# Moving weight loads to the K queue in a fixed order, and keeping V loads in order with the exps, in a grouped-query attention kernel

## The chip, the cores and the metric

The kernel runs on one core of a Trainium2 chip. The metric is the device time of one execution in microseconds. Several executions are measured, and each has a state, fast or slow (here slow means more than 1.5% above the fastest run of the same kernel). Times are medians of all runs. A profile is one further look at one execution; its span is about 2 us shorter than the time reported for it (757.7 against 759.44 us before).

## The reference, cut to what matters

Two independent problems A and B of the same shape are computed, and their outputs are concatenated.

```python
B, Sq, D = 16, 80, 576                 # batch, queries, model width
Hq, Hkv, Sk, Dh = 32, 16, 512, 128     # two query heads share a K/V head
q = (x @ wq).reshape(B, Sq, Hq, Dh).transpose(0, 2, 1, 3)
k, v = repeat(k_cache, 2, axis=1), repeat(v_cache, 2, axis=1)
p = softmax(einsum("bhqd,bhkd->bhqk", q, k) * Dh ** -0.5)
o = einsum("bhqk,bhkd->bhqd", p, v)
out = o.transpose(0, 2, 1, 3).reshape(B, Sq, Hq * Dh) @ wo
```

Everything is bf16. Each problem reads 33.6 MB of K, as much of V, 4.7 MB of wq and 4.7 MB of wo.

## The kernel before: the parts that matter

The work is cut into 128 *units*. A unit is one batch entry and four K/V heads (512 KB of K, 512 KB of V). Eight units make an *octet*, which shares one quarter of wq and of wo (1.18 MB each). There are 16 octets: 0 to 7 are problem A, 8 to 15 are B. In program order a unit is: K loaded with a transposing DMA (from SP), V loaded (from ScalarE, "ACT"), V converted by GpSimd ("POOL"), scores on TensorE, exp on ScalarE, P·V on TensorE, transposes, output projection.

Every operation is recorded with a key (the intended position, 16 key steps to a unit) and its reads and writes. A planner then simulates all engines with estimated costs and fixes the order of each engine's instructions. The program gives each engine its instructions in that order. In the timelines below, what stands behind a slow DMA issue of the same engine waits for it: ScalarE's first table load comes at 25.38 us, when its last DMA issue of that stretch ends.

```python
NK = 5      # K buffers
NV = 2      # V input buffers
NVP = 4     # converted V buffers
...
    def _simulate(self, ops, alldeps):
        ...     # at each step: the engine that can go first takes the ready op with the lowest key
            if o.dsem is not None:                       # a DMA
                free[e] = t0 + self.ISSUE[e]
                kind = o.name.rstrip("0123456789.")
                link = max(link, free[e] + 0.6) + self.XFER[kind]
                end, lat = link, 1.3
...
        # K and V loads of unit U
        t_k = T0 - 16.0 * (NK - 1) - LA + 1.5 if U >= NK else -790.0 + 3 * U
        t_p = T0 - 24.0 if U >= 2 else -700.0 + U
        t_v = t_p - 16.0 * NV + 1.0 if U >= NV else -789.0 + 3 * U
        add("sp", t_k, em_ldk, writes=[R(("kT", ks), U)], dsem="d_k%d" % ks, name="ldk%d" % U)
        add("act", t_v, em_ldv, writes=[R(("Vi", vs), U)], dsem="d_v%d" % vs, name="ldv%d" % U)
        add("pool", t_p, em_vp, reads=[R(("Vi", vs), U), ...], writes=[R(("V", vps), U)], name="vp%d" % U)
...
        # weights: wq in three pieces, wo in two, per problem and quarter q, on ScalarE
                    add("act", t_w + dt * part, em_ldwa, ...)
            add("sp" if (prob, q) == (0, 0) else "act", t_w + 2 * dt, em_ldwb, ...)
                add("act", t_wo + 24.0 * part, em_ldwo, ...)
```

A weight load has no predecessor while its buffer is free. The planner therefore places it as early as the engine's simulated time allows, whatever its key says.

Of the kernel before, what the change touches and what calls it, by code (L numbers as in the profile page):

```python
# [616 lines left out]
class _Plan(_Sched):  # L617
# [13 lines left out]
    def plan(self):  # L631
        ops = sorted(self.ops, key=lambda o: (o.key, o.seq))
        last_w, readers, cur_ver = {}, {}, {}
        alldeps = {}
        for op in ops:
            deps = {}
            for r, ver in op.reads:
                w = last_w.get(r)
                assert w is not None, ("read of never-written resource", r, op.name)
                assert cur_ver[r] == ver, ("version mismatch", r, cur_ver[r], ver, op.name)  # L640
                deps[id(w)] = w
            for r, ver in op.writes:
                w = last_w.get(r)
                if w is not None:
                    deps[id(w)] = w
                for rd in readers.get(r, ()):
                    deps[id(rd)] = rd
            deps.pop(id(op), None)
            for r, ver in op.reads:
                readers.setdefault(r, []).append(op)  # L650
            for r, ver in op.writes:
                last_w[r] = op
                readers[r] = []
                cur_ver[r] = ver
            alldeps[id(op)] = list(deps.values())
            for d in deps.values():
                if d.eng == "pe" and op.eng == "pe":
                    continue
                op.deps.append(d)
                d.signals = True  # L660
            if op.dsem is not None:
                op.signals = True
        order = self._simulate(ops, alldeps)
        for i, op in enumerate(order):
            op.key, op.seq = float(i), i
        counts = {}
        for op in order:
            if not op.signals:
                continue
            ck = ("d", op.dsem) if op.dsem is not None else ("e", op.eng)  # L670
            counts[ck] = counts.get(ck, 0) + (16 if op.dsem is not None else 1)
            op.sidx = (ck, counts[ck])
        self.totals = counts
        known = {}
        for op in order:
            kq = known.setdefault(op.eng, {})
            need = {}
            for d in op.deps:
                ck, v = d.sidx
                if need.get(ck, (0, None))[0] < v:  # L680
                    need[ck] = (v, d)
            for ck, (v, d) in sorted(need.items(), key=lambda kv: -kv[1][1].key):
                if kq.get(ck, 0) >= v:
                    continue
                op.waits.append((ck, v))
                for k2, v2 in d.clock.items():
                    if kq.get(k2, 0) < v2:
                        kq[k2] = v2
            if op.signals:
                op.clock = dict(kq)  # L690
                op.clock[op.sidx[0]] = op.sidx[1]
        self.sorted_ops = order
        return order

    def _simulate(self, ops, alldeps):
        ndep = {id(o): len(alldeps[id(o)]) for o in ops}
        users = {}
        for o in ops:
            for d in alldeps[id(o)]:
                users.setdefault(id(d), []).append(o)  # L700
        ready = {id(o): 0.0 for o in ops}
        cand = {}
        for o in ops:
            if not ndep[id(o)]:
                cand.setdefault(o.eng, []).append(o)
        free = {e: 0.0 for e in ("pe", "act", "dve", "pool", "sp")}
        link = 0.0
        order = []
        self.pe_idle = []
        lastdma = {}  # L710
        while any(cand.values()):
            best = None
            for e, cs in cand.items():
                if not cs:
                    continue
                t0 = max(free[e], min(ready[id(o)] for o in cs))
                if best is None or t0 < best[0]:
                    best = (t0, e)
            t0, e = best
            cs = cand[e]  # L720
            o = min((o for o in cs if ready[id(o)] <= t0 + 1e-9), key=lambda o: (o.key, o.seq))
            cs.remove(o)
            if e == "pe" and t0 > free[e] + 0.02:
                self.pe_idle.append((t0 - free[e], t0, o.name))
            o.clock = t0
            order.append(o)
            if o.dsem is not None:
# [4 lines that stand above are left out]
            else:  # L732
                free[e] = t0 + self.cost[id(o)]
                end, lat = free[e], self.LAT.get(e, 0.1)
            for u in users.get(id(o), ()):
                same = u.eng == e and o.dsem is None
                t = t0 if same and e == "pe" else end + (0.06 if same else lat)
                ready[id(u)] = max(ready[id(u)], t)
                ndep[id(u)] -= 1
                if not ndep[id(u)]:  # L740
                    cand.setdefault(u.eng, []).append(u)
        self.span = max(free.values())
        assert len(order) == len(ops)
        for o in order:
            o.clock = None
        return order


def bass_concat_heads__gqa_block_cached__gqa_block_cached__near_ridge_kernel(
# [61 lines left out]
    def R(res, ver):  # L811
        return (res, ver)
# [39 lines left out]
    for ph in range(NPH):  # L852
        prob, half = divmod(ph, NPP)
# [38 lines left out]
    for prob in range(2):  # L892
        wq_ap, wo_ap = probs[prob][3], probs[prob][4]
        u_p = prob * NPP * SUPP
        for q in range(NOCT):
            if prob == 0:
                t_w = (-799.0, -785.0, 16.0 * 5 + 10.0, 16.0 * 12 + 10.0)[q]
            else:
                t_w = 16.0 * (u_p - SUPP + 8 * q + 4) + 10.0
            dt = (0.1 if q == 1 else 0.4) if prob == 0 and q < 2 else 6.0  # L900
            if (prob, q) == (0, 0):
                for hp in range(4):
                    def em_ldwp(e, wq_ap=wq_ap, hp=hp):
                        src = wq_ap[0:512, hp * 256:(hp + 1) * 256]
                        return e.dma_start(wq_sb[:, 0, 0:4, hp * 256:(hp + 1) * 256],
                                           src.rearrange("(c p) n -> p c n", p=128))

                    add("act", t_w + 0.1 * hp, em_ldwp, writes=[R(("wq", 0, p_, hp), 0) for p_ in range(2)],
                        dsem="d_wp%d" % hp, name="ldwp%d" % hp)
            else:  # L910
                for part, (c0, c1) in enumerate(((0, 2), (2, 4))):
                    def em_ldwa(e, wq_ap=wq_ap, q=q, c0=c0, c1=c1):
                        src = wq_ap[c0 * 128:c1 * 128, q * 1024:(q + 1) * 1024]
                        return e.dma_start(wq_sb[:, q, c0:c1, :], src.rearrange("(c p) n -> p c n", p=128))  # L914

                    add("act", t_w + dt * part, em_ldwa, writes=[R(("wq", q, part, hp), prob) for hp in range(4)],
                        dsem="d_wq%d" % q, name="ldwa%d.%d.%d" % (prob, q, part))

            def em_ldwb(e, wq_ap=wq_ap, q=q):
                return e.dma_start(wq_sb[64:128, q, 4, :], wq_ap[512:576, q * 1024:(q + 1) * 1024])  # L920

            add("sp" if (prob, q) == (0, 0) else "act", t_w + 2 * dt, em_ldwb,
                writes=[R(("wq", q, 2, hp), prob) for hp in range(4)], dsem="d_wq%d" % q, name="ldwb%d.%d" % (prob, q))
            for part in range(2):
                h0 = 8 * q + 4 * part

                def em_ldwo(e, wo_ap=wo_ap, h0=h0):
                    src = wo_ap[h0 * 128:(h0 + 4) * 128, :]
                    return e.dma_start(wo_sb[:, h0:h0 + 4, :], src.rearrange("(h p) n -> p h n", p=128))  # L929

                t_wo = 16.0 * (u_p + 8 * q) - 40.0 if u_p + q else 14.0
                add("act", t_wo + 24.0 * part, em_ldwo, writes=[R(("wo", q, part), prob)],
                    dsem="d_wo%d" % q, name="ldwo%d.%d.%d" % (prob, q, part))


    for k in range(2 * NPH * NOCT):
        goct, c = divmod(k, 2)
        ph, q = divmod(goct, NOCT)
# [270 lines left out]
    ops = S.plan()  # L1209
# [79 lines left out]
```

## Time and profile before

Median 758.85 us of three runs (757.82 to 769.3, the last one slow). The profiled run's span is 757.7 us.

To see where time goes, the span is cut at the first P·V matmul of every eighth unit. The P·V line of the trace has 16 matmuls per unit, so the cut times are start times read from it. An octet that nothing disturbs takes about 41.5 us.

| stretch of the span, us | before |
|---|---|
| start to unit 0's first P·V | 39.0 |
| octet 0 | 53.4 |
| octets 1, 2 | 41.7, 41.8 |
| octets 3 to 8 | 43.8, 45.4, 49.3, 43.5, 48.9, 47.4 |
| octets 9 to 14 | 41.5, 42.4, 43.2, 41.4, 42.4, 41.6 |
| from unit 120 to the end | 51.0 |

The page's busy table and its slices. Each digit is the busy share of one fortieth of the span in tenths; PEclk is the granted TensorE clock in tenths.

```profile
PE 700.5 (92%) x9508; PEld 593.8 (78%) x9508; DVE 386.2 (51%) x961; ACT 382.2 (50%) x732; POOL 244.8 (32%) x136
...
PE   4387999999999897999989989999999999999986
...
ACT  0163565555555553554535546555555566555561
...
PEclk8589999999999998999999989999999999999999
DMA  9998999999999999999999989998999998989941
```

TensorE is the engine that is full, except in the first four slices and in a handful near the middle. ScalarE does nothing in the first slice and little in the second.

The timeline of the first 45 us (start, duration, engine and line, what; in brackets the idle time before it and its releaser). "ACTq" and "SPq" are issues by ScalarE's and SP's sequencers.

```profile
9.08 39.28 SPq L1022 DMA_TRANSPOSE kT<-in_A_k_cache_dram  x4
9.13 7.30 ACTq L929 DMA_DIRECT2D wo_sb<-in_A_wo_dram  x3
...
16.46 3.40 ACTq L914 DMA_DIRECT2D wq_sb<-in_A_wq_dram  x2
...
21.96 3.39 ACTq L914 DMA_DIRECT2D wq_sb<-in_A_wq_dram  x2
25.38 1.28 ACT L960 ACT_TABLE_LOAD   x1 [25.38 <-issue]
...
26.67 0.43 ACT L960 CAST qT<-ps 128x320 bf16<-128x320 f32 x1
...
27.16 5.25 PE L953 MATMUL ps<-xT,wq_sb 128*128 128x320 bf16 x20 [16.66 <-ACT qT L960]
```

ScalarE issues weights (and two V loads) until 25.4 us. Only then does it copy the first query projection out of PSUM (the tile `ps`, which the matmuls write), and TensorE has stood for 16.66 us. Meanwhile four K issues on SP take 39 us together.

From the waits view (total us, times, longest) and, second, the chain of waits (start, duration, what):

```profile
POOL v_sb L1029 <- DMA v_in<-in_A_v_cache_dram: 123.8, 28, 30.8
...
ACT P L994 <- POOL v_sb L1029: 26.3, 8, 5.5
...
PE ps L989 <- ACT P L994: 22.1, 14, 4.4
...
PE ps L953 <- ACT qT L960: 16.7, 1, 16.7
```

```profile
281.27 14.84 DMA v_in<-in_A_v_cache_dram
...
379.18 10.40 DMA v_in<-in_A_v_cache_dram
...
423.46 12.69 DMA v_in<-in_B_v_cache_dram
```

In the middle the chain runs through V loads that land after 10 to 15 us (the median for V is 5.6 us). In octets 3 to 8 TensorE's gaps add up to 16.0 us, of which 15.8 us are waits for ScalarE's exps ("ACT P" in the waits view of 175.9 to 454.2 us). ScalarE itself stands until GpSimd has converted a late V (26.3 us in eight waits), because its next instruction is the V load into that buffer. Within about 1 us of the end of each of the three longest gaps (299.1, 392.7 and 439.2 us) a stretch begins in which the granted TensorE clock is 0.50 (298.3, 393.8 and 438.2 us); these are 17.1 us in all, and TensorE is busy in 15.2 of them. In such a stretch, from the start of one group to the start of the next, five projection matmuls took 1.34 us and eight output matmuls 1.92 us (299.94 to 303.20 us); at full clock they took 0.68 and 0.98 us (306.65 to 308.31 us). That is about half the work, so the stretches cost another 7.6 us (an estimate: half of the 15.2 busy us).

### The profile page before, as it was taken

How to read it: one execution, taken by the hardware profiler on the slowest of the kernel's cores; microseconds unless marked ns; L12 is line 12 of the kernel's file. 1: busy time of each engine (PE TensorE's matmuls, PEld its weight loads, DVE VectorE, ACT ScalarE, POOL GpSimd, SP SyncE). 2: the span in 40 equal slices, each digit the busy share in tenths (PEclk: the TensorE clock that was granted, in tenths of full speed). 3: DMA queues.
4: the chain of work that ended last, by engine and by line, in shares of the span. 5: the costliest groups of instructions: out<-in, count | busy, mean ns of one | idle time of the engine just before them, and what ended most of it. 6: DMA issues, size and time to landing. Idle time of an engine off the chain costs nothing.

```text
span 757.7 us, 21437 instructions
## 1 busy us (share of the span) xinstructions
PE 700.5 (92%) x9508; PEld 593.8 (78%) x9508; DVE 386.2 (51%) x961; ACT 382.2 (50%) x732; POOL 244.8 (32%) x136
## 2 busy tenths in 40 slices
PE   4387999999999897999989989999999999999986
PEld 3265788888888786887878868888888888888874
DVE  1023456555655443555646525555665545655564
ACT  0163565555555553554535546555555566555561
POOL 4012353322432322323324224323433324332230
PEclk8589999999999998999999989999999999999999
DMA  9998999999999999999999989998999998989941
GB/s 259 301 303 175 214 235 199 212 215 200 204 230 259 183 212 229 216 266 259 253 245 233 219 190 189 225 205 201 187 202 202 216 229 196 199 207 204 200 93 38
DMA packets 355142, 161.08 MB, mean 213 GB/s; under 512 B 269536, under 2 KB 350944, under 8 KB 355040
## 3 DMA queue, kind: packets, MB, share of 16 engines
q1 hardware_dynamic: 272528, 73.75, 56.2%
q10 hardware_dynamic: 82512, 85.86, 41.5%
q8 instruction: 77, 1.26, 0.7%
q14 instruction: 25, 0.20, 0.1%
HBM read 89.52 MB, written 2.95 MB: 122 GB/s over the span
## 4 chain that ended last, share of the span: by engine, by line
PE 79%; DMA 8%; ACTq 5%; ACT 2%; POOL 2%; DVE 2%; issue 1%
PE ps L953 21%; PE ps L1133 19%; PE ps L989 17%; PE ps L1050 14%; DMA v_in<-in_A_v_cache_dram 7%; PE ps L1083 4%; PE ps L1097 3%; ACTq L929 2%; POOL v_sb L1029 2%; ACT P L994 2%; DMA v_in<-in_B_v_cache_dram 2%; ACTq L914 1%; PE ps L1098 1%; DVE qT L960 1%; ACTq L1026 1%; PE ps L877 1%
## 5 line engine op out<-in xcount | busy, mean ns | idle before, releaser
L994 ACT ACTIVATE P<-ps 128x480 bf16<-128x480 f32 (+1 forms) x683 | 363.6, 569 | 296.4 <-PE ps L989 246.3
L1029 POOL COPY v_sb<-v_in 128x2048 bf16<-128x2048 bf16 x128 | 240.5, 1896 | 491.3 <-PE ps L1083 311.1
L989 PE MATMUL ps<-qT,kT 128*128 128x160 bf16 x2048 | 235.0, 234 | 22.9 <-ACT P L994 22.1
L953 PE MATMUL ps<-xT,wq_sb 128*128 128x320 bf16 x1280 | 219.2, 304 | 22.5 <-ACT qT L960 16.7
L960 DVE CAST qT<-ps 128x320 bf16<-128x320 f32 x248 | 121.4, 490 | 153.3 <-PE ps L953 152.9
L1050 PE MATMUL ps<-v_sb,P 128*128 128x129 bf16 x2048 | 196.4, 222 | 0.9 <-POOL v_sb L1029 0.9
L989 PEld LDWEIGHTS ps<-qT,kT 128*128 128x128 bf16 x2048 | 155.6, 98 | 44.4 <-ACT P L994 28.1
L1133 PE MATMUL ps<-wo_sb,oT 128*128 128x288 bf16 x1280 | 184.9, 288 | 0.5 <-DVE flag L1195 0.3
L953 PEld LDWEIGHTS ps<-xT,wq_sb 128*128 128x128 bf16 x1280 | 117.6, 99 | 58.7 <-ACT qT L960 17.9
L1050 PEld LDWEIGHTS ps<-v_sb,P 128*128 128x128 bf16 x2048 | 146.2, 99 | 6.3 <-POOL v_sb L1029 1.2
L1133 PEld LDWEIGHTS ps<-wo_sb,oT 128*128 128x128 bf16 x1280 | 122.2, 98 | 30.8 <-DVE oT L1102 0.6
L1102 DVE COPY oT<-ps 128x640 bf16<-128x640 bf16 x128 | 62.1, 486 | 27.5 <-PE ps L1098 27.3
L1063 DVE RECIPROCAL rinv<-ps 128x3 f32<-128x3 f32 (+1 forms) x216 | 38.1, 177 | 71.8 <-PE ps L1050 42.6
L1067 DVE TENSOR_TENSOR oA<-ps,rinv 128x384 bf16<-128x384 f32 x128 | 71.3, 557 | 4.3
L1148 DVE TENSOR_TENSOR acc<-ps,acc 128x288 f32<-128x288 f32 x80 | 36.6, 458 | 61.7 <-PE ps L1133 61.7
L1097 PE MATMUL ps<-ident,oA 128*128 128x128 bf16 x384 | 42.7, 220 | 2.4 <-DVE oT L1102 1.6
L1083 PE MATMUL ps<-v_sb,P 128*32 128x129 bf16 x2048 | 38.7, 223 | 0.0
L1097 PEld LDWEIGHTS ps<-ident,oA 128*128 128x128 bf16 x384 | 30.8, 99 | 7.9 <-DVE oT L1102 2.0
L1083 PEld LDWEIGHTS ps<-v_sb,P 128*32 128x32 bf16 x2048 | 30.7, 97 | 5.5 <-ACT P L994 0.8
L1154 DVE TENSOR_TENSOR osb<-ps,acc 128x288 bf16<-128x288 f32 x40 | 18.3, 458 | 32.3 <-PE ps L1133 32.3
L1142 ACT COPY acc<-ps 128x288 f32<-128x288 f32 x40 | 16.0, 399 | 29.5 <-PE ps L1133 24.7
L1097 PE MATMUL ps<-ident,oZ 128*128 128x128 bf16 x128 | 28.2, 220 | 0.0
(27 smaller groups left out, 152.4 us busy)
## 6 DMA issues: line engine op xcount, KB each, us to landing
v_in<-in_A_v_cache_dram ACTq DMA_DIRECT2D x64, 512.0 KB, 5.7
v_in<-in_B_v_cache_dram ACTq DMA_DIRECT2D x64, 512.0 KB, 5.5
wo_sb<-in_A_wo_dram ACTq DMA_DIRECT2D x8, 576.0 KB, 14.2
wo_sb<-in_B_wo_dram ACTq DMA_DIRECT2D x8, 576.0 KB, 8.1
wq_sb<-in_B_wq_dram ACTq DMA_DIRECT2D x8, 512.0 KB, 7.3
wq_sb<-in_A_wq_dram ACTq DMA_DIRECT2D x6, 512.0 KB, 12.5
out_dram<-osb SPq DMA_DIRECT2D x20, 144.0 KB, 3.0
xs<-in_A_x_dram SPq DMA_DIRECT2D x4, 288.0 KB, 5.4
```

What stands on the lines that cost most here:

```text
L953: last = e.matmul(ps[:, bank, 0:320], lhsT=wq_sb[:, q, ck, i * 128:(i + 1) * 128], rhs=xT[:, c, ck, :], start=(ck == 0), stop=(ck == 4))
L960: return e.copy(dst, src) if ev == "act" else e.tensor_copy(dst, src)
L989: last = e.matmul(ps[:, sbk, c * 160:(c + 1) * 160], lhsT=kT[:, U % NK, j, g * 128:(g + 1) * 128], rhs=qT[:, k % 2, bl % 4, g * 160:(g + 1 ...
L994: return e.activation(P[:, psl, 0:k, :], ps[:, sbk, 0:k * 160].rearrange("p (c n) -> p c n", c=k), AF.Exp, scale=SCALE)
L1029: return e.tensor_copy(v_sb[:, vps, :, 0:128], v_in[:, vs, :, :].rearrange("p g (j d) -> p (g j) d", j=4))
L1050: last = e.matmul(ps[:, bank, off:off + 129], lhsT=pap(16 * U + 4 * g + j, 0, 128), rhs=v_sb[:, vps, 4 * g + j, 0:129], start=(j == 0), st ...
L1063: return e.reciprocal(ri, ps[:, bank, 128:128 + OP_ * (nt - 1) + 1:OP_])
L1067: return e.tensor_tensor(dst, src, ri.unsqueeze(2).to_broadcast([128, nt, 128]), AluOpType.mult)
L1083: last = e.matmul(ps[32 * g:32 * g + 32, OY, w_ * OP_:w_ * OP_ + 129], lhsT=pap(16 * U_ + 4 * g + j, 128, 160), rhs=v_sb[:, U_ % NVP, 4 * ...
L1097: e.transpose(psb[:, TB, g * 160:g * 160 + 128], src, ident[:])
L1102: return e.tensor_copy(oT[:, goct % 2, :, bl * SQ:(bl + 1) * SQ], psb[:, TB, 0:640].rearrange("p (h s) -> p h s", s=SQ))
L1133: last = e.matmul(ps[:, bank, 0:DC], lhsT=oT[:, goct % 2, hi, r * 128:(r + 1) * 128], rhs=wo_sb[:, 8 * q + hi, c3 * DC:(c3 + 1) * DC], sta ...
```

## The change

The intent: ScalarE should not spend its time issuing weights, V should not queue behind weights, and the loads should go out at the places that their keys intend. Three things are done. All weights except the four first wq pieces move to SP's queue. SP's DMAs keep their key order. A V load may not be planned before the exp (or other ScalarE work) that precedes it by key.

```diff
+        prev = {}
+        for op in ops:                       # ops in key order
+            p = prev.get(op.eng)
+            if op.dsem is not None and op.eng in ("act", "sp"):
+                if p is not None:
+                    alldeps[id(op)].append(p)
+                if op.eng == "sp":
+                    prev[op.eng] = op
+            elif op.eng == "act":
+                prev[op.eng] = op
         order = self._simulate(ops, alldeps)
 ...                                          # an issue is ready when the op before it starts
-                t_w = (-799.0, -785.0, 16.0 * 5 + 10.0, 16.0 * 12 + 10.0)[q]
+                t_w = (-799.0, -783.5, 16.0 * 5 + 10.0, 16.0 * 12 + 10.0)[q]
-            dt = (0.1 if q == 1 else 0.4) if prob == 0 and q < 2 else 6.0
+            dt = 0.1 if prob == 0 and q < 2 else 6.0
 ...
-                    add("act", t_w + dt * part, em_ldwa, ...
+                    add("sp", t_w + dt * part, em_ldwa, ...
-            add("sp" if (prob, q) == (0, 0) else "act", t_w + 2 * dt, em_ldwb,
+            add("sp", t_w + 2 * dt, em_ldwb,
-                add("act", t_wo + 24.0 * part, em_ldwo, ...
+                add("sp", t_wo + 24.0 * part, em_ldwo, ...
```

More of the change, by code (lines that the diff above doesn't have):

```diff
@@ L699, in _simulate @@
             for d in alldeps[id(o)]:
-                users.setdefault(id(d), []).append(o)
+                users.setdefault(id(d), []).append((o, o.eng == d.eng and o.dsem is not None))
         ready = {id(o): 0.0 for o in ops}
@@ L734, in _simulate @@
                 end, lat = free[e], self.LAT.get(e, 0.1)
-            for u in users.get(id(o), ()):
+            for u, issue in users.get(id(o), ()):
                 same = u.eng == e and o.dsem is None
-                t = t0 if same and e == "pe" else end + (0.06 if same else lat)
+                if issue:
+                    t = t0
+                else:
+                    t = t0 if same and e == "pe" else end + (0.06 if same else lat)
                 ready[id(u)] = max(ready[id(u)], t)
@@ L914, in em_ldwa @@
                         return e.dma_start(wq_sb[:, q, c0:c1, :], src.rearrange("(c p) n -> p c n", p=128))
-                    add("act", t_w + dt * part, em_ldwa, writes=[R(("wq", q, part, hp), prob) for hp in range(4)],
+                    add("sp", t_w + dt * part, em_ldwa, writes=[R(("wq", q, part, hp), prob) for hp in range(4)],
                         dsem="d_wq%d" % q, name="ldwa%d.%d.%d" % (prob, q, part))
@@ L931, in bass_concat_heads__gqa_block_cached__gqa_block_cached__near_ridge_kernel @@
                 t_wo = 16.0 * (u_p + 8 * q) - 40.0 if u_p + q else 14.0
-                add("act", t_wo + 24.0 * part, em_ldwo, writes=[R(("wo", q, part), prob)],
+                add("sp", t_wo + 24.0 * part, em_ldwo, writes=[R(("wo", q, part), prob)],
                     dsem="d_wo%d" % q, name="ldwo%d.%d.%d" % (prob, q, part))
```

## The prediction

The sum is 29 less 2, plus 21, plus 1, about 50 us.

> **What bounds the kernel now.** TensorE: the page has PE busy 92% of a 757.7 us span. Cutting the span at every eighth unit's first P·V matmul (times of the trace) gives an undisturbed octet of 41.5 us; 16 of them are 664 us. So about 94 us is start, tail and disturbance:
> - Start: unit 0's first P·V matmul comes at 39.0 us, unit 8's at 92.4 (53.4 us for that octet). The timeline shows ScalarE issuing DMAs without a break until 25.4 us, its first cast at 26.7, and TensorE idle 16.7 us waiting for it ("ACT qT", one wait, in the waits view). The issues are all eight halves of wo A and wq A, up to 6.8 us each in a backed-up queue, although only octet 0's are needed by then.
> - K is starved as well. By packets, the ScalarE queue moved 210-310 GB/s between 16 and 48 us and the K queue 40-70; K1 to K4 landed at 26.9, 40.4, 48.2, 52.2 us. Alone, the K queue moves about 240 GB/s. [...]
> - Middle: octets 3 to 8 take 43.8, 45.4, 49.3, 43.5, 48.9, 47.4 us, 29 us above 41.5. B's weights are issued then, before V loads on the same queue. The chain of waits has V landings of 14.8, 10.4 and 12.7 us at 281, 379 and 423 us, against a median of 5.6; the granted clock then falls to 0.75-0.91 for some us.
>
> **What changes.** No arithmetic and no bytes. Weights, except the four first wq A pieces, go behind K in SP's queue, at fixed places, spread over units 3 to 28 (A) and 36 to 87 (B). ScalarE issues V only, and a V load may not be planned before the exp preceding it.
>
> **Cost by step.**
> 1. ScalarE is free at about 5.5 us. Query projection ends near 13, K0 and V0 land near 14 as now; first P·V about 17.5 us (now 39.0).
> 2. Octet 0 about 46 us (K, V, wq1 and wo0 compete, clock still recovering): unit 8 near 64, gain 29 us. On the critical path.
> 3. Octets 1 and 2 now carry A's weights. Estimate from trace rates: K 2.2 + V 1.7 us per unit, 31 us per octet, plus 7.6 us of weights: 39 of 41.5 us. Fits barely: lose 2 us.
> 4. Octets 3 to 8: V no longer queues behind weights; K has five buffers and absorbs them. Excess 29 to about 8: gain 21 us.
> 5. The rest about unchanged; V loads more evenly spaced, perhaps 1 us.
>
> Sum about 50 us: **predicted 708 us, 80% range 695 to 727**. Chances: faster by over 2% 0.95, within 2% 0.04, slower 0.01.
>
> **Right if:** ScalarE's first cast is before 9 us, the long TensorE wait for it is gone, first P·V is at 15-22 us; K1 to K4 land by 35 us; no V landing in the middle exceeds about 9 us; V landings fall from 9% of the chain to under 4%; octets 3 to 8 are under 44 us each; granted clock averages above 0.98.
>
> **Wrong if:** SP's fixed order blocks at its head: an output store or a weight load waiting for its buffer holds back K (TensorE then waits for kT, K landings late), or K waits behind 1.2 MB of weights in the first octet (octet 0 above 50 us); if DMA is saturated in octets 1 to 3 (above 44 us); or if the middle's excess came from the phase change (stores, x loads) rather than weights, when step 4 gives under 10 us.

## The result and the profile after

The changed kernel takes 721.69 us (median of 4 runs, 719.22 to 727.89), the kernel before 758.94 us. The ratio is 0.9526 (95% interval 0.9443 to 0.9609). A ratio here is always the mean time of one kernel's fast runs over that of the other's fast runs of the same rounds, so it is not quite the ratio of the medians quoted. A second measurement of both on another chip (`c1_after_again` below) gave 0.949 (0.9441 to 0.9539).

| stretch, us | before | predicted | after |
|---|---|---|---|
| start to unit 0's first P·V | 39.0 | 17.5 | 19.3 |
| octet 0 | 53.4 | 46 | 54.0 |
| octets 1, 2 together | 83.5 | 85.5 | 81.8 (40.0, 41.8) |
| octets 3 to 8 together | 278.3 | 257 | 257.2 (42.6, 42.4, 41.6, 43.8, 45.5, 41.4) |
| octets 9 to 14 together | 252.4 | about the same | 252.6 |
| from unit 120 to the end | 51.0 | the same | 52.7 |

The 40 us come from two places: 19.7 us before the first P·V, and 21.1 us in octets 3 to 8. The other stretches differ by 0.2 to 1.7 us and nearly cancel.

The page, the same rows:

```profile
PE 691.4 (96%) x9508; PEld 591.3 (82%) x9508; DVE 385.8 (54%) x961; ACT 382.3 (53%) x732; POOL 245.3 (34%) x136
...
PE   7789999999999999999999999999999999999985
...
ACT  1655545545556654554555665555545665555551
...
PEclk9899999999999999999999999999999999999998
DMA  9999999999999999999999999999999999999921
```

The holes in the middle of the PE row are gone. The start is better but not full.

The timeline of the first 60 us:

```profile
5.55 1.28 ACT L973 ACT_TABLE_LOAD   x1 [5.55 <-issue]
...
8.43 0.43 ACT L973 CAST qT<-ps 128x320 bf16<-128x320 f32 x1 [1.59 <-PE ps L966]
...
16.96 0.45 PE L890 MATMUL ps<-ident,xs 128*128 128x128 bf16 x5 [1.98 <-DMA xs<-in_A_x_dram]
...
20.39 1.09 SPq L927 DMA_DIRECT2D wq_sb<-in_A_wq_dram  x2
...
22.05 12.42 SPq L1035 DMA_TRANSPOSE kT<-in_A_k_cache_dram  x3
...
32.84 0.37 PE L1002 MATMUL ps<-qT,kT 128*128 128x160 bf16 x3 [3.31 <-DMA kT<-in_A_k_cache_dram]
```

ScalarE is free at 5.55 us. The first K issues are no longer starved, but K3 now stands behind wq's second quarter and TensorE waits 3.31 us for it.

The waits view, and the chain of waits around 270 to 340 us:

```profile
POOL v_sb L1042 <- DMA v_in<-in_A_v_cache_dram: 121.7, 33, 10.2
...
ACT P L1007 <- POOL v_sb L1042: 15.9, 6, 3.7
...
PE ps L1002 <- ACT P L1007: 5.6, 7, 1.6
...
PE ps L1002 <- DMA kT<-in_A_k_cache_dram: 3.3, 1, 3.3
...
PE ps L1146 <- DMA wo_sb<-in_A_wo_dram: 1.4, 1, 1.4
```

```profile
274.24 12.29 DMA v_in<-in_A_v_cache_dram
...
314.79 9.56 DMA v_in<-in_A_v_cache_dram
```

The one 16.7 us wait has become several of 1 to 3 us, for transfers that were not in time. Late V landings have not become rarer: after the first 50 us, ten V loads took over 9 us to land, against six before. The longest fell from 14.8 to 12.8 us. These two landed at 286.5 and 324.4 us, just before TensorE's gaps of 1.1 us at 289.6 (octet 6, 43.8 us) and 1.5 us at 327.4 (octet 7, 45.5 us). What fell is what such landings cost: TensorE's gaps in octets 3 to 8 fell from 16.0 to 3.3 us, and there is no half-clock stretch left in them. With the estimate of 7.6 us for the clock, this makes 20.3 us, nearly the whole gain of the middle (21.1 us).

### The profile page after: what moved, and what is told of

Its sections match the earlier page's. It is cut to its first block, busy times and chain, and to the rows that moved or that the text cites. A ratio compares the mean times of both kernels' runs of the same rounds, so it can differ in the third digit from the quotient of the medians.

```text
span 717.6 us, 21433 instructions
## 1 busy us (share of the span) xinstructions
PE 691.4 (96%) x9508; PEld 591.3 (82%) x9508; DVE 385.8 (54%) x961; ACT 382.3 (53%) x732; POOL 245.3 (34%) x136
## 4 chain that ended last, share of the span: by engine, by line
PE 86%; DMA 6%; SPq 3%; DVE 1%; ACT 1%; POOL 1%; issue 0%; ACTq 0%
PE ps L966 21%; PE ps L1146 21%; PE ps L1002 18%; PE ps L1063 15%; PE ps L1096 5%; DMA v_in<-in_A_v_cache_dram 4%; PE ps L1110 4%; SPq L1035 2%; DMA kT<-in_A_k_cache_dram 1%; ACT P L1007 1%; DMA wo_sb<-in_A_wo_dram 1%; PE ps L1111 1%; POOL v_sb L1042 1%; PE ps L890 1%; SPq L878 0%
## 5 line engine op out<-in xcount | busy, mean ns | idle before, releaser
L1002 PE MATMUL ps<-qT,kT 128*128 128x160 bf16 x2048 | 231.4, 234 | 9.4 <-ACT P L1007 5.6
L966 PE MATMUL ps<-xT,wq_sb 128*128 128x320 bf16 x1280 | 215.8, 300 | 2.3 <-DMA wq_sb<-in_A_wq_dram 1.7
L1063 PE MATMUL ps<-v_sb,P 128*128 128x129 bf16 x2048 | 192.6, 221 | 0.6 <-issue 0.6
L1063 PEld LDWEIGHTS ps<-v_sb,P 128*128 128x128 bf16 x2048 | 143.9, 98 | 5.8 <-issue 0.7
L1076 DVE RECIPROCAL rinv<-ps 128x3 f32<-128x3 f32 (+1 forms) x216 | 38.1, 176 | 66.2 <-PE ps L1096 32.7
```

The costliest lines, as they stand in the source:

```text
L966: last = e.matmul(ps[:, bank, 0:320], lhsT=wq_sb[:, q, ck, i * 128:(i + 1) * 128], rhs=xT[:, c, ck, :], start=(ck == 0), stop=(ck == 4))
L1002: last = e.matmul(ps[:, sbk, c * 160:(c + 1) * 160], lhsT=kT[:, U % NK, j, g * 128:(g + 1) * 128], rhs=qT[:, k % 2, bl % 4, g * 160:(g + 1 ...
L1063: last = e.matmul(ps[:, bank, off:off + 129], lhsT=pap(16 * U + 4 * g + j, 0, 128), rhs=v_sb[:, vps, 4 * g + j, 0:129], start=(j == 0), st ...
L1076: return e.reciprocal(ri, ps[:, bank, 128:128 + OP_ * (nt - 1) + 1:OP_])
```

## The experiments

All of them are edits of the changed kernel unless said otherwise. The runs fall into three, each on a chip of its own, with the kernel before in the same rounds; so they are compared by their ratio to it.

| run | ratio to before | 95% interval | median, us |
|---|---|---|---|
| the change | 0.9526 | 0.9443 to 0.9609 | 721.69 |
| c1_after_again (control) | 0.949 | 0.9441 to 0.9539 | 724.07 |
| e1_B_on_act | 0.976 | 0.9643 to 0.9877 | 738.23 |
| e2_A_on_act | 0.9829 | 0.9731 to 0.9926 | 744.5 |
| e3_V_free | 0.9742 | 0.965 to 0.9835 | 737.62 |
| e4_SP_free | 0.9818 | 0.9717 to 0.9919 | 741.23 |
| f1_wq1_late | 0.949 | 0.944 to 0.9541 | 723.94 |
| f2_NV3 | 0.9499 | 0.9451 to 0.9547 | 723.98 |
| g1_all_act_fixed | 0.9625 | 0.9574 to 0.9675 | 734.05 |
| h0_start | 0.9587 | 0.9551 to 0.9623 | 727.59 |
| h1_best | 0.9439 | 0.9398 to 0.948 | 717.98 |
| b1_bytes (wrong) | 0.9476 | 0.9434 to 0.9518 | 719.97 |
| g2_before_NV3 | 0.9903 | 0.9847 to 0.9958 | 754.76 |

### First set: undo one part at a time

The theory was that the queue matters: A's weights on ScalarE cost the start, B's weights in front of V cost the middle. The rival was that the new order rules do the work.

**e1: B's weights back on ScalarE, freely placed.**

```diff
-add("sp", t_w + dt * part, em_ldwa, ...
+add("act" if prob else "sp", t_w + dt * part, em_ldwa, ...    # the other two loads alike
+if op.dsem is not None and op.eng == "act" and op.name[:3] == "ldw": continue   # no order rule for them
```

> The changed kernel, but problem B's weight loads issued on ScalarE's queue again, at places the planner chooses freely, as before; A's weights stay on SP at fixed places. Theory (weights in front of V loads on one queue cause the middle's excess): octets 3 to 8 lie about 20 us above the changed kernel's (8 us excess back to about 25), V landings of 12 us or more, time 737 to 746 us; first P.V stays near 19 us. Rival (the middle was slow for the phase change's stores and x loads, and improved through the fixed order of V loads): octets 3 to 8 as in the changed kernel, time 719 to 727 us.

Measured: 738.23 us, first P·V at 19.1 us. Octets 3 to 8: 42.7, 42.4, 49.4, 43.9, 51.8, 41.4. The chain of waits between 265 and 375 us, with its longest pieces:

```profile
261.44 15.08 DMA v_in<-in_A_v_cache_dram
...
357.19 14.50 DMA v_in<-in_A_v_cache_dram
```

The theory holds for octets 5 and 7: they lose 7.8 and 6.3 us, and V landings of 15 us are back. It does not hold for octets 3, 4 and 8. They stay as in the changed kernel, although B's weights are again in V's queue. Of the 21 us gained in the middle, about 14 go with B's weights by this one profile; 7 must come from another part of the change. Two limits: the edit gives B's weights back both their old queue and their free placement, so it does not say which of the two counts; and octet 7 scatters. With B's weights on SP it took 45.2 to 50.4 us in the profiles of e2, e4, f1, h0 and b1, while octet 5 took 41.5 to 41.6 in all of them. Only octet 5's 7.8 us are clear of this scatter.

**e2: A's weights back on ScalarE, freely placed.** The mirror image of e1's edit.

> The changed kernel, but problem A's weight loads issued on ScalarE's queue again, freely placed; B's stay on SP. Theory (the start was lost to ScalarE issuing A's weights): first P.V back near 39 us, first cast near 26 us, octet 0 about 53 us, octets 3 to 8 as in the changed kernel, time 738 to 744 us. Rival (the start gains mainly by V loads kept behind exps): first P.V near 20 us and time under 727 us.

Measured: 744.5 us. First P·V at 39.8 us, octet 0 52.6 us, octets 3 to 8 together 260.0 us. ScalarE's first cast is late again:

```profile
26.06 1.28 ACT L975 ACT_TABLE_LOAD   x1 [26.06 <-issue]
...
27.35 0.42 ACT L975 CAST qT<-ps 128x320 bf16<-128x320 f32 x1
```

As the theory said: the gain before the first P·V comes from A's weights not being issued by ScalarE at the start.

**e3: V loads without the order rule.**

```diff
+if op.dsem is not None and op.eng == "act": continue
 if op.dsem is not None and op.eng in ("act", "sp"):
```

> The changed kernel without the rule that a V load follows the exp before it; SP's fixed order stays. Theory (the rule is worth little, the queue is what counts): within 4 us of the changed kernel, 718 to 727 us. Rival (the rule evens out V loads and is worth a good part of the middle's 21 us): 730 us or more, with octets 3 to 8 above 44 us each.

Measured: 737.62 us, ratio 0.9742; its fast runs are 734.9 to 739.4 us, those of the control 718.0 to 728.2. The theory's expectation fell: the rule is worth 2 to 3 per cent of the time of before, about as much as each of the other parts.

**e4: SP without its fixed order.**

```diff
+if op.dsem is not None and op.eng == "sp": continue
 if op.dsem is not None and op.eng in ("act", "sp"):
```

> The changed kernel without SP's fixed order: weights are on SP, but the planner issues them as early as a buffer is free, so all of A's weights go out between K3 and K4. Theory (the fixed places are needed because weights delay K in the same queue): first P.V near 19 us as in the changed kernel, but K4 lands after 50 us instead of 35 and unit 8 starts 10 to 20 us later; then octets 1 and 2 without weights at 40 to 41 us; time 730 to 742 us. Rival (only the queue matters, the order does not): 719 to 727 us.

Measured: 741.23 us. First P·V at 18.7 us, but octet 0 takes 70.9 us and unit 8 starts at 89.6 instead of 73.3. All of A's weights beyond wq's first two quarters are issued between K4 and K5 (the expectation had said between K3 and K4): K4 lands at 33.8 us and K5 only at 64.7. TensorE meets the stop below, shown by the timeline. Octets 3 to 8 together are 255.0 us, as good as in the changed kernel.

```profile
64.88 0.56 PE L1004 MATMUL ps<-qT,kT 128*128 128x160 bf16 x3 [11.63 <-DMA kT<-in_A_k_cache_dram]
```

So moving the weights to SP without fixing their places would have given back nearly all of the start's gain: 16 us of it.

### Second set: is it the queue or the places, and what is wrong with octet 0?

**c1: the change again, as a control.**

> The changed kernel unaltered, as a control on this chip. Both theories: 719 to 728 us, ratio to before 0.945 to 0.960.

Measured: 0.949, five fast runs from 718.0 to 728.2 us. This kernel scatters by more than one per cent from run to run.

**g1: all weights on ScalarE, at the changed kernel's places.** The three `add("sp", ...)` of the weights become `add("act", ...)` (except wq's very first small piece); both order rules stay.

> The changed kernel with all weights issued on ScalarE, but at the same planned places (spread over the run, kept in order with the exps), instead of on K's queue. Theory (the queue matters: a V load behind weights lands late, and ScalarE then stands): first P.V stays near 19 us, since the flood is gone, but octets 1, 2, 5 and 7 each lose 3 to 8 us; 735 to 748 us. Rival (only the spreading in time matters): 719 to 728 us.

Measured: 734.05 us, ratio 0.9625, beside 0.949 of the control. The fall was smaller than the theory said (734 against at least 735). Spreading and ordering the loads gives 3.75 of the 5.1 per cent with no change of queue; the queue adds about 1.3 per cent on top. With e4, where the queue and the V rule without fixed places on SP were worth 1.8 per cent, this says that the places (with the order rules that hold the loads to them) are the larger part.

**f1: wq's second quarter after K4.** `t_w` of that quarter goes from -783.5 to -776.0.

> The changed kernel with the three loads of wq A's second quarter put behind K4 instead of between K2 and K3. In the changed kernel K3 landed at 32.7 us, 4 us behind those weights, and TensorE stood 3.3 us before unit 3's scores. Theory (octet 0 was longer than predicted because weights sit in front of K): K3 lands near 28 us, the 3.3 us stop goes, unit 8 starts 3 to 5 us earlier, time 3 to 5 us below the control. Rival (octet 0 is limited by DMA bytes, so a new order only moves the stop): unit 8 within 1.5 us of the control and another stop of about 3 us appears.

Measured: 0.949, the control's ratio. K3 landed at 26.2 us and the stop for K3 went, exactly as the edit intended. A new stop appeared, shown by the timeline:

```profile
47.33 0.90 PE L1146 MATMUL ps<-wo_sb,oT 128*128 128x288 bf16 x3 [5.00 <-DMA wo_sb<-in_A_wo_dram]
```

Unit 8 started at 74.2 us (73.3 in the changed kernel). The rival was right: the stop moved.

**f2: three V buffers.** `NV = 3`; to make room in SBUF, `NOA` goes from 4 to 3 and `NSB` from 3 to 2.

> The changed kernel with three V input buffers instead of two (room made by NOA 3 for 4 and NSB 2 for 3). Theory (what stalls TensorE in the middle is ScalarE standing at a V load whose buffer is not free, because the V before landed late): ScalarE's waits for the V conversion fall from 15.9 us to under 5, octets 6 and 7 (43.8, 45.5) to under 43, the V-free stop at 91 us goes, time 4 to 8 us below the control. Rival (V itself comes too late, whoever issues it): octets 6 and 7 stay and the time is within 2 us of the control.

Measured: 0.9499, no gain. ScalarE's wait for the V conversion fell from 15.9 us to none. Unit 8 started at 69.6 us instead of 73.3, but the planner had also moved less work forward (octet 0 holds 90 projection matmuls instead of 115), and by unit 24 only 1.2 us were left (153.9 against 155.1). Octet 6 was 42.2 us, but octet 7 was 52.4. In the timeline:

```profile
338.96 6.39 SPq L1035 DMA_TRANSPOSE kT<-in_A_k_cache_dram  x1
...
345.39 1.09 SPq L878 DMA_DIRECT2D xs<-in_B_x_dram  x2
...
348.93 0.72 PE L890 MATMUL ps<-ident,xs 128*128 128x128 bf16 x5 [5.75 <-DMA xs<-in_B_x_dram]
```

SP stood with a slow K issue for 6.39 us, x of problem B came behind it, and TensorE stood 5.75 us for x. This is the head-of-line cost of a fixed order on one queue. The run has a single profile, so it shows that this can happen, not how often.

### Third set: places or bytes, and a better version

**h0: a new order of SP's first loads.** x's second half before K0; K0 to K4 next; then wq's second quarter, and the two parts of wo ahead of K5 and K6.

```diff
-t_ld, t_x = (-800.0, -788.0)[c], ...
+t_ld, t_x = (-800.0, -798.5)[c], ...
-t_w = (-799.0, -783.5, ...)[q]
+t_w = (-799.0, -776.0, ...)[q]
-t_wo = 16.0 * (u_p + 8 * q) - 40.0 if u_p + q else 14.0
+t_wo = 16.0 * (u_p + 8 * q) - 40.0 if u_p + q else -10.0
```

> The changed kernel with a new order of SP's first loads: x's second half ahead of K0, then K0 to K4, then wq A's second quarter and both parts of wo A's first quarter ahead of K5 and K6. It takes away the three stops seen in octet 0 (2 to 3.6 us for x, 3 to 4 us for K3, 1.4 to 5 us for wo). Theory A (octet 0 is a matter of places): unit 8 starts 5 to 8 us earlier than 73 to 75 us, ratio to before 0.938 to 0.944. Theory B (octet 0 is limited by the DMA bytes it needs, so stops only move): unit 8 within 2 us of 73 us, ratio 0.946 to 0.952.

Measured: 0.9587, worse than the control, and the intervals do not overlap. Unit 8 started at 75.8 us. The stops for x, K3 and wo were gone; in their place stood one of 2.8 us for unit 0's scores, one of 4.3 us for wq and two of 1.9 and 4.2 us before P·V, which begin at 74 and 82 us. Theory A (it is only a matter of places) falls for this order.

**b1: fewer bytes.** wq A's second and wo A's first quarter are loaded at a quarter of their bytes, and GpSimd zeroes the rest beforehand; the result is wrong (relative error 0.30).

```diff
+c1, n = (c0 + 1, 512) if less else (c1, 1024)     # less: problem A, q == 1
+nh = 1 if (wo_ap is probs[0][4] and h0 < 8) else 4
```

> Wrong result on purpose: the changed kernel with wq A's second quarter and wo A's first quarter loaded at a quarter of their bytes (2.2 MB become 0.55 MB; GpSimd zeroes the rest before), same instructions and places. Theory B (octet 0 is short of DMA bytes): K3 lands 3 us earlier, the wo stop goes, unit 8 starts 4 to 7 us earlier than 73 to 75 us. Theory A (places, not bytes): unit 8 moves by under 2 us.

Measured: octet 0 was 50.6 us instead of 54.0, and unit 8 started at 70.3 instead of 73.3; the total ratio 0.9476 cannot be told from the control's. The shift of 3 us lies between the two expectations. K3 came at 30.6 us and the stop for K3 was gone; 1.8 us for wo stayed. The shift is still there at unit 24 (151.4 against 155.1 us); octet 7 took it back (50.4 against 45.5). So bytes account for a part of the 8 us by which octet 0 exceeds the predicted 46, about 3 us by this one look.

**g2: the kernel before with three V buffers.** Same `NV`, `NOA` and `NSB` as in f2, on the unchanged kernel.

> The kernel before with three V input buffers (same room made), nothing else of the change. Theory (the middle's excess is ScalarE standing at a V load for a buffer that a late V holds): its waits for the V conversion fall from 26 us to under 8 and octets 3 to 8 lose at least 12 of their 29 us excess; time 738 to 750 us. Rival (late V and K themselves stop TensorE): under 5 us gained, 752 us or more.

Measured: 754.76 us, ratio 0.9903. ScalarE's wait for the V conversion (26.3 us in before) was gone altogether, yet octets 3 to 8 still took 271.4 us, against 278.3. TensorE's waits named other things:

```profile
PE ps L1133 <- DVE osb L1154: 4.5, 2, 3.3
...
PE ps L989 <- DMA kT<-in_A_k_cache_dram: 3.4, 2, 1.9
...
PE ps L989 <- DMA kT<-in_B_k_cache_dram: 1.2, 1, 1.2
```

By the total the rival was right. But the test is not clean: the 4.5 us for `osb` are waits for a free output buffer, held by an output store that was itself late (`osb`'s writer stood 7.0 us for the store, in two waits), and the edit cut these buffers (`NSB`) from 3 to 2; before had no such wait. Octet 5 did fall, from 49.3 to 42.3 us, while octets 6, 7 and 8 took 47.3, 48.2 and 46.4. What is shown is that octets can be slow without ScalarE standing at a V load, when K and output stores are late. How much of before's excess that standing makes stays open.

**h1: h0, three V buffers, and the second x load of a later phase two units earlier** (`(13, 7)` becomes `(13, 9)` in that load's key).

> The previous kernel with three V buffers (room as in the NV 3 run) and the second x load of each later phase two units earlier in SP's order. With three V buffers alone, the ScalarE wait went but 5.75 us were lost at 343 us, where x of problem B stood behind a slow K on SP. Theory: octets 3 to 8 all under 43.5 us, no stop for x, ratio 0.938 to 0.946. Rival (late landings keep turning up somewhere else): ratio 0.947 to 0.952.

Measured: 717.98 us, ratio 0.9439. Octets 3 to 8 were 42.7, 42.4, 41.6, 41.5, 43.8 and 43.0 us, and there was no stop for x in them. Unit 8 started at 62.5 us, about where the prediction had put it (64), and octet 0 took 41.8. Part of this is work that the planner no longer moved forward (90 projection matmuls in octet 0, 129 score matmuls; the changed kernel has 115 and 150), and octet 1 took 48.1 with 4.0 us of waits for K. At unit 24, 2.6 us were left (152.5 against 155.1). Its four fast runs were 714.8 to 718.4 us, but two of six runs were slow (730 and 738). The interval overlaps the control's, and the control ran on another chip. Whether h1 beats the changed kernel is not settled.

## Why the prediction was right or wrong, point by point

**What bounds the kernel, and steps 1 and 4 in size: right.** First P·V was said at 17.5 us and came at 19.3; octets 3 to 8 were said to keep 8 us of excess and kept 8.2 (257.2 minus six times 41.5); about 4 us of that are the extra work of octets 3, 4 and 7 (in the run `h1_best`, in which TensorE has no gap in them, they take 42.7, 42.4 and 43.8 us) and could not have gone. e2 shows the cause of the first, since putting A's weights back on ScalarE put first P·V back to 39.8.

**Step 2, the term that was mis-sized: "Octet 0 about 46 us ... gain 29 us".** Octet 0 took 54.0 us, and the gain up to unit 8 was 19.1 us (92.4 to 73.3). Unit 8 was said to start near 64 us; the 9 us are most of the 13.7 us by which the median missed 708. The total stayed inside the predicted range because that range was wide, not because octet 0 was foreseen. The trace gives these parts, worked out against an undisturbed octet of 41.5 us:
- TensorE's idle gaps inside octet 0 add up to 6.3 us, among them K3 (3.3) and wo (1.4).
- Work was moved forward. Octet 0 holds 115 projection matmuls instead of 80, 21 more score matmuls and 32 fewer output matmuls. At 0.68 us for five, 0.21 for three and 0.98 for eight, this is 2.3 us more. (In the kernel before, octet 0 held 95, 6 more and 32 fewer: 1.5 us less than undisturbed.) Octet 1, with 55 projection matmuls, is short by it: 40.0 us.
- The granted clock was at half for 4.8 us of octet 0 (17.3 to 20.7 and 34.4 to 37.8 us), an estimated 2.4 us at most. In 0.2 us windows over the whole span of both profiles, the granted clock is 0.5 or 1.0, with other values only where a stretch begins or ends. The half-clock stretches are 3.4, 6.8 or 17.1 us long, except the cut one at the end. What starts and ends one is not shown.

f1 and h0 show that the idle part is not cured by these two orders alone (7.0 and 6.4 us of gaps in octet 0). h0's order with a third V buffer (h1) had only 1.7 us of gaps in octet 0, but 4.0 in octet 1; which of its edits does this was not tested. In b1 3 us go with the bytes. The rest of octet 0's excess is not explained further.

**Step 4's cause: half right.** The prediction put all 21 us down to V no longer queueing behind weights. e1 shows about 14 us that go with B's weights, in octets 5 and 7, of which octet 5's 7.8 are clear of scatter; it does not separate the queue from the fixed places. The other 7 us came from something else in the change. The V landings themselves stayed late (ten over 9 us against six); TensorE's gaps and half-clock stretches behind them are what went.

**Step 5, "V loads more evenly spaced, perhaps 1 us": wrong in size.** Without the rule for V loads the time rises to 737.62 us. Why the rule is worth so much stays open. Standing at the V load was my explanation. f2 and g2 do not support it as the main cause, since with that wait gone they gained nothing and one per cent, but both also gave up output buffers, and g2 lost 4.5 us to that.

**Step 3, octets 1 and 2 lose 2 us: wrong, harmless.** They took 81.8 instead of 83.5 us. A's weights did fit beside K and V, and the 1.5 us by which octet 1 was short go with the work moved forward.

**The signs named.** First cast before 9 us: 8.43. K1 to K4 by 35 us: 21.0, 24.7, 32.7 and 34.6. Clock above 0.98: 0.99. Octets 3 to 8 all under 44: octet 7 was 45.5. No V landing above 9 us in the middle: wrong, 12.8 and 12.3 us were seen for loads issued at 268 and 274 us. V's share of the chain "under 4%": 4.1% for A's V alone, so missed.

**The fear named, a fixed order that blocks at its head: real here.** Its sign "octet 0 above 50 us" was met: octet 0 took 54.0 us, and K3 stood behind wq's second quarter, which cost TensorE 3.31 us. Moving those weights (f1) only moved the stop, so the fixed order is not shown to be the whole reason. f2 has the fear once in the middle, at 5.75 us. The opposite risk was larger and was not priced: e4 shows that without the fixed order on SP the weights block K, and 16 us are lost in octet 0.

The parts do not add. Taking back any one of four parts (e1 to e4) costs 2 to 3.5 per cent, and their sum is far above the 5 per cent that the whole change gives. A likely reading, argued and not shown, is that one late transfer can hide behind another.

## What to carry to other kernels

When loads crowd the start, first ask which of them the first units need, and put the others at fixed places later; here that was worth more than the choice of queue (ratio 0.9625 with the places alone, 0.9818 with the new queue but free places on it, 0.949 to 0.953 with both). Do not let an engine with compute work issue loads into a queue that backs up: in before, single issues held ScalarE for up to 6.76 us, and its first cast came at 26.7 us. Before moving a load to remove one stop, check whether the DMA has room; otherwise the stop can turn up at the next tile, as it did in f1 (3.3 us for K3 became 5.0 us for wo).

## What the traces show of the loads

- Issuing the loads took an engine's time. In before, ScalarE was tied up until 25.4 us, with single issues of up to 6.76 us while earlier loads were still on their way. The place of a load in one queue or the other also mattered: 0.9625 against 0.949 at the same keys (g1 and the control).
- The stream of K's transposes lost against plain loads. In before, between 16 and 48 us, both queues moved the same number of packets (6358 for K, 6356 for ScalarE's loads), but 1.61 MB against 8.31 MB, so K's packets had 253 bytes on average and the others 1307. In 4 us windows that is 30 to 68 GB/s beside 212 to 312 GB/s. With the other queue empty, K's moved 220 (62 to 66 us) and 229 GB/s (311 to 315 us).
- An issue of a 512 KB K load held SP's sequencer for 1.3 us at least, 3.4 (A) and 3.0 us (B) in the median, and 12.0 us at most, in the kernel before.
- The landing time of equal loads scattered. The V loads of the changed kernel, all of 512 KB, landed after 3.8 to 13.6 us.
